# Where the loads of wo, wout and the spatial weights stand in the SyncE queue

## The chip, the cores and the metric

The kernel runs on one core of a Trainium2 chip. A core has TensorE (PE) for matrix products, VectorE (DVE), ScalarE (ACT) and GpSimd (POOL) for work on elements, and SyncE (SP), which here does nothing but issue DMA transfers. Each engine works through its own list of instructions in order; semaphores make one engine wait for another or for the landing of a transfer. The metric is the device time of one execution in microseconds; the median of several runs is compared.

## The reference

Two branches over the same x (2048 tokens of 512) are mixed with a gate for each token:

```python
q = (x @ wq) as 32 heads of 16          # keys and values: one head of 16, shared by all
scores = q k^T * 16 ** -0.5;  p = softmax(scores);  a = (p v) @ wo

z = gelu(x @ w_in)                      # 1376 wide, split into halves of 688
z1, z2 = z[..., :688], layernorm(z[..., 688:])
g = w_sp @ z2 + b_sp                    # over the tokens, w_sp is 2048 x 2048
b = (z1 * g) @ w_out

gate = sigmoid((x * gate_w).sum(-1))
out = gate * a + (1 - gate) * b
```

## The kernel before, in words

**The attention** goes by 32 units: a chunk of 512 queries and four heads each. For a tile of 128 keys TensorE computes scores of 512 queries into a bank of PSUM (tile `ps`), from `QA` and `KA`. `KA[:, 0]` holds the keys as they come from the projection, `KA[:, 1]` the same keys moved by 16 partitions, which serves the other heads of a pair. ScalarE turns most score banks into probabilities with an exponential (`P`, line 804). The rest go to VectorE and GpSimd, which replace the exponential by a polynomial (`UW`, lines 816, 823, 829); part of that polynomial is a term that is linear in the keys, so that for those tiles sums over V (`SVB`) and over products of K and V (`KTV`) can be used. TensorE then multiplies `P` and `UW` with `V`. The three engines are loaded about equally by this.

**The gMLP** is fitted into the same stream on TensorE: `win` (the first gMLP weights) gives z1 and z2, ScalarE applies the gelu, VectorE the layer norm; then `wT`, the transposed spatial weights, in four loads of 512 columns; then `wout` for the gMLP's result and `wo` for that of the attention, both added in one bank.

**What sets the order.** When the program is built, a planner plays the engines' work through with costs and due times of its own and writes out a fixed list of instructions for each engine. `op(engine, ...)` appends to the list; what an operation reads and writes determines its waits. SP's list, too, is in the order in which the planner calls `op("sp", ...)`. SP takes its list strictly in that order: where an entry waits, all behind it wait.

**The DMA helpers around the change.** `ld_K1(c, t)` (line 305) issues the copy of one chunk of 512 keys from `KA[:, 0]` to `KA[:, 1]` (line 306); it waits only for VectorE, which writes the chunk. `sp_dma` (line 282) issues a load and, with `chain=True`, makes it wait for the landing of the load that was issued by `sp_dma` before. `ld_win` loads win, `ld_bsp` (line 314) a row of 512 numbers of b_sp into `bspz`, `ld_wo` (line 317) issues eight loads of 64 KB. `ld_rest` (line 344) issues the load of wout, two small loads for the rest of wout, and `ld_wT(0)`: four transposing loads of 128 rows of w_sp each (line 339). The groups of these lists that TensorE computes have a `done` function, which the planner calls when the group is through and which appends what follows: `done` of `g_K` (the projection of the keys of one chunk, in the order of chunks 0, 3, 2, 1) appends that chunk's key copy; `done` of `g_KTV` (the sums over products of K and V) appends four small copies that spread the sums into `KTV` (lines 590 to 592), and behind them the loads of wo, wout and wT. The sums over V come as a group of their own, `g_SV`, right beside it.

In this program the group g_KTV is through before the last key chunk, chunk 1.

Of the kernel before, what the change touches and what calls it, by code (L numbers as in the profile page):

```python
# [78 lines left out]
class Prog:  # L79
# [12 lines left out]
    def op(self, eng, fn, r=(), w=(), chan=None, dma=0, after=(), tag=""):  # L92
        if dma:
            chan = "%s_d%d" % (self.name, self.ndma)
            self.ndma += 1
        else:
            chan = "%s_%s%s" % (self.name, eng, chan or "")
        o = Op(eng, fn, chan, dma, tag)
        deps = []
        for k in r:  # L100
            d = self.lastw.get(k)
            if d is not None:
                deps.append((d, True))
        for k in w:
            d = self.lastw.get(k)
            if d is not None:
                deps.append((d, True))
            for d in self.readers.get(k, ()):
                deps.append((d, False))
        for d in after:  # L110
            deps.append((d, True))
        if eng == "pool" and self.ops[eng] and not self.ops[eng][-1].dma and not dma:
            deps.append((self.ops[eng][-1], True))
        seen = set()
        for d, raw in deps:
            if d.eng == eng and not d.dma:
                if eng == "pe":
                    continue
            if id(d) in seen:
                continue  # L120
            seen.add(id(d))
            d.need = True
            o.deps.append(d)
        for k in r:
            self.readers.setdefault(k, []).append(o)
        for k in w:
            self.lastw[k] = o
            self.readers[k] = []
        self.ops[eng].append(o)
        return o  # L130
# [39 lines left out]
def build_kernel(nc, x_d, wq_d, wk_d, wv_d, wo_d, win_d, wsp_d, bsp_d, wout_d, gw_d, out_d):  # L170
    es = ExitStack()
    with es:
        block = es.enter_context(nc.Block())

        def sb(name, shape, dt):
            return es.enter_context(nc.sbuf_tensor(name, shape, dt))
# [3 lines left out]
        def bank(b, n=512, off=0):  # L180
            return ps[:, 512 * b + off:512 * b + off + n]
# [4 lines left out]
        def bkey(b):  # L186
            return ("bk", b)
# [23 lines left out]
        wo = sb("wo", [128, 4, D], B16)  # L211
# [70 lines left out]
        def sp_dma(fn, r=(), w=(), n=16, chain=True, tag=""):  # L282
            o = op("sp", fn, r=r, w=w, dma=n, after=[dprev[0]] if chain and dprev[0] is not None else [], tag=tag)
            dprev[0] = o
            return o
# [19 lines left out]
        def ld_K1(c, t):  # L305
            op("sp", lambda q: q.dma_start(KA[16:128, 1, 512 * c:512 * c + 512], KA[0:112, 0, 512 * c:512 * c + 512]),
               r=[("K0", c)] + (["K0a"] if c == XO[0] else []), w=[("K1", c)], dma=16, tag="K1")
            spc["free"] = max(spc["free"], t) + 650.0
            T[("K1", c)] = spc["free"] + 2300.0

        def ld_win():
            sp_dma(lambda q: q.dma_start(win[:], win_d.rearrange("(dt p) n -> p dt n", p=128)), w=["win"])

        def ld_bsp(tc):
            sp_dma(lambda q: q.dma_start(bspz[0:1, tc % 2, :], bsp_d[512 * tc:512 * tc + 512].rearrange("(one t) -> one t", one=1)), w=[("bspz", tc % 2)])
# [20 lines left out]
        def ld_wT(tc):  # L336
            for k in range(4):
                r0 = 512 * tc + 128 * k
                sp_dma(lambda q, r0=r0, tc=tc, k=k: q.dma_start_transpose(wT[:, :, 128 * k:128 * k + 128], wsp_d[r0:r0 + 128, :]),
                       w=[("wT", k)], tag="wT")  # L340
            if tc > 0:
                ld_bsp(tc)

        def ld_rest():
            sp_dma(lambda q: q.dma_start(wout[:, 0:5, :], wout_d[0:640, :].rearrange("(ft p) n -> p ft n", p=128)), w=["wout"])
            for h in range(2):
                sp_dma(lambda q, h=h: q.dma_start(wout[64 * h:64 * h + 48, 5 + h, :], wout_d[640:688, :]), w=["wout5"])
            ld_wT(0)
# [24 lines left out]
        def mm(dst, lhsT, rhs, start, stop, r, w, tp=None, chan=None, tag=""):  # L373
            def fn(t):
                if tp is None:
                    return t.matmul(dst, lhsT, rhs, start=start, stop=stop)
                return t.matmul(dst, lhsT, rhs, start=start, stop=stop, tile_position=tp)  # L377
            return op("pe", fn, r=r, w=w, chan=chan, tag=tag)
# [6 lines left out]
        def fm(b, n, off, lhsT, rhs, start, stop, r, tag):  # L385
            for q in range(4):
                mm(ps[32 * q:32 * q + 32, 512 * b + off:512 * b + off + n], lhsT[:, 32 * q:32 * q + 32], rhs, start, stop, r, [bkey(b)],
                   tp=(0, 32 * q), tag=tag)
# [12 lines left out]
        def when(*keys):  # L401
            t = 0.0
            for k in keys:
                if k not in T:
                    return None
                t = max(t, T[k])
            return t
# [33 lines left out]
        def qt(x):  # L441
            t = x[2]() if callable(x[2]) else x[2]
            return 1e12 if t is None else t

        def g_K(c, lo=0, hi=512, b=BM):
            key = "K0a" if c == XO[0] and lo == 0 else ("K0", c)

            def piece(dt):
                return lambda: fm(b, hi - lo, 0, wk_rep[:, dt, :], xT[:, dt, 512 * c + lo:512 * c + hi], dt == 0, dt == 3, ["wk_rep", ("x", c)], "K")

            def ev():
                op("dve", lambda v: v.tensor_copy(KA[:, 0, 512 * c + lo:512 * c + hi], bank(b, hi - lo)), r=[bkey(b)], w=[key], tag="Kev")

            def done(t):
                T[key] = t
                if hi == 512 and c == XO[1]:
                    ld_K1(c, t)
                    ld_K1(XO[0], t)
                elif hi == 512 and c == XO[2]:
                    ld_K1(c, t)  # L460
                    ld_win()
                elif hi == 512 and c == XO[3]:
                    ld_K1(c, t)
                    ld_bsp(0)
                if all(("K0", c2) in T for c2 in range(4)) and hi == 512:
                    for c2 in range(4):
                        early.append(g_k2(c2))
            return Group([((hi - lo) / 2.4 + 2.6, piece(dt)) for dt in range(4)], [(68.0 + (hi - lo) / 0.96, ev)], lambda: when(("x", c)), done, bank=b, tag="K")
# [105 lines left out]
        def g_KTV():  # L574
            n0 = NKT - NMAX

            def piece(k, e):
                def f():
                    for q in range(4):
                        o = 512 * BM + 32 * NMAX * e  # L580
                        mm(ps[32 * q:32 * q + 32, o:o + 32 * (k + 1)], KN[:, k, e, :], V1[:, n0 + k:n0 + k + 1, :].broadcast_to([128, k + 1, 32]), k == NMAX - 1, k == 0,
                           ["KN", ("V", (n0 + k) // 4)], [bkey(BM)], tp=(0, 32 * q), tag="KTV")
                return f

            def ev():
                op("dve", lambda v: v.tensor_scalar(KF, bank(BM, 64 * NMAX).rearrange("p (e k w) -> p k e w", e=2, w=32), Q_C1, None, ALU.mult),
                   r=[bkey(BM), ("z1", 5)], w=["KF"], tag="KTVev")

            def done(t):
                for q in range(4):  # L590
                    op("sp", lambda d, q=q: d.dma_start(KTV[32 * q:32 * q + 32, :, :, q, :], KF[32 * q:32 * q + 32, :, :, :]),  # L591
                       r=["KF", ("z1", 5)], w=[("KTV", q)], dma=16, after=[o_ktv], tag="KTV")
                T["KTV"] = t + 6000.0
                sp_dma(ld_wo, w=["wo"], n=128)
                ld_rest()
            return Group([(26.0 + 13.4 * k, piece(k, e)) for e in range(2) for k in range(NMAX - 1, -1, -1)], [(C_EV, ev)], lambda: when(("V", 2), ("V", 3)), done, tag="KTV")

        def gate():
# [351 lines left out]
        for i, c in enumerate(XO):  # L950
# [3 lines left out]
        free = {"pe": 6600.0, "act": 7000.0, "dve": 6800.0}  # L954

        first = deque([g_K(XO[0], 0, 128), g_Q(0, DBK[0]), g_K(XO[0], 128, 512), g_V(XO[0], BO), g_K(XO[1]), g_V(XO[1], BO), g_K(XO[2]), g_V(XO[2]),
                       g_K(XO[3]), g_V(XO[3])])
        early = deque()
# [964 lines left out]
def bass_gated_mix__grouped_kv_mqa__mixer_gmlp__prompt_kernel(  # L1923
    nc, A_x, A_wq, A_wk, A_wv, A_wo, B_x, B_w_in, B_w_sp, B_b_sp, B_w_out, gate_w, out,
):
    build_kernel(nc, A_x, A_wq, A_wk, A_wv, A_wo, B_w_in, B_w_sp, B_b_sp, B_w_out, gate_w, out)
# [29 lines left out]
```

## Time and profile before

| | us |
|---|---|
| median of 3 runs | 748.63 (748.27 to 748.7) |
| the profiled execution, its own time | 748.98 |
| its span, first to last instruction | 747.2 |
| PE busy | 714.1 (96%) |
| DVE busy | 704.9 (94%) |
| ACT busy | 708.7 (95%) |
| POOL busy | 471.3 (63%) |
| mean granted TensorE clock | 0.985 of full speed |

Times in the rows of the profile are microseconds from the span's start, unless marked ns. A row of the timeline has start, duration, engine, line, operation, output and input and the count; a bracket at the end is the idle time of the engine before it and what ended it. SPq is SP's queue with its DMA issues; the duration of such a row is that of issuing, not of the transfer. The granted clock is the share of full speed that TensorE was allowed.

### The profile page before, as it was taken

What the parts mean: (1) busy time and instruction counts of PE and PEld (TensorE: products, weight loads), DVE (VectorE), ACT (ScalarE), POOL (GpSimd) and SP (SyncE); (2) the same over time, 40 slices, a digit from 0 to 9 for tenths busy, and PEclk for the clock granted to TensorE, in tenths of its full rate; (3) what the DMA queues carried; (4) which work ended last, traced back from release to release, by engine and by line L of the source; (5) the groups of instructions that cost most, each with busy time, mean ns of one, the idle gap of its engine ahead of it and who ended that gap; (6) DMA issues with size and microseconds to landing.
All of it is one profiled execution on the core that took longest, in us unless ns stands there. A gap on an engine that the chain in (4) does not pass through costs nothing.

```text
span 747.2 us, 21846 instructions
## 1 busy us (share of the span) xinstructions
PE 714.1 (96%) x9048; PEld 210.7 (28%) x9048; DVE 704.9 (94%) x1035; ACT 708.7 (95%) x757; POOL 471.3 (63%) x440
## 2 busy tenths in 40 slices
PE   8927999999999999999999999999999999999996
PEld 3302322232432222322222232222223222222322
DVE  6934999999999999999999999999999999999996
ACT  5936999999999999999999999999999999999995
POOL 5520376766037876667777677756767776677772
PEclk9977999999999999999999999999999999999999
DMA  8441000000001000150000105000001510000101
GB/s 156 133 113 36 1 2 2 2 2 1 3 2 27 4 2 2 30 100 9 9 1 2 38 2 128 9 10 2 1 2 23 109 36 8 2 2 2 31 1 33
DMA packets 59810, 20.12 MB, mean 27 GB/s; under 512 B 54804, under 2 KB 59192, under 8 KB 59704
## 3 DMA queue, kind: packets, MB, share of 16 engines
q1 hardware_dynamic: 57448, 18.36, 11.0%
q8 instruction: 73, 1.20, 0.6%
q10 hardware_dynamic: 2256, 0.30, 0.2%
q14 instruction: 33, 0.27, 0.1%
HBM read 3.38 MB, written 2.10 MB: 7 GB/s over the span
## 4 chain that ended last, share of the span: by engine, by line
PE 69%; DVE 11%; ACT 10%; DMA 4%; issue 4%; SPq 1%; ACTq 0%; DVEq 0%
PE ps L377 69%; ACT P L804 9%; DVE UW L816 4%; DVE bst L635 2%; DMA wT<-in_B_w_sp_dram 2%; DVE UW L823 2%; DVE UW L829 1%; DMA wout<-in_B_w_out_dram 1%; DVE z L649 1%; DMA xT<-in_A_x_dram 1%; SPq L591 0%; SPq L318 0%; DMA KA<-KA 0%; ACT z L629 0%; DMA wo<-in_A_wo_dram 0%
## 5 line engine op out<-in xcount | busy, mean ns | idle before, releaser
L804 ACT ACTIVATE P<-ps 128x1024 bf16<-128x1024 f32 (+1 forms) x738 | 683.5, 1185 | 27.0 <-PE ps L377 26.7
L829 POOL TENSOR_TENSOR UW<-UW 128x512 f16<-128x512 f16 (+1 forms) x300 | 375.4, 1251 | 156.1 <-DVE UW L829 63.8
L816 DVE TENSOR_SCALAR UW<-ps 128x512 f16<-128x512 f32 (+1 forms) x423 | 351.0, 851 | 2.6 <-PE ps L377 1.9
L377 PE MATMUL ps<-QA,KA 32*128 32x512 bf16 x2048 | 313.6, 385 | 23.2 <-DMA KA<-KA 18.1
L377 PE MATMUL ps<-P,V 128*32 128x512 bf16 x1488 | 204.7, 386 | 0.4 <-issue 0.3
L823 DVE TENSOR_TENSOR UW<-UW 128x2048 f16<-128x2048 f16 (+1 forms) x176 | 177.9, 1011 | 1.3
L377 PEld LDWEIGHTS ps<-QA,KA 32*128 32x128 bf16 x2048 | 86.1, 91 | 325.6 <-ACT P L804 151.7
L377 PE MATMUL ps<-UW,VW 128*32 128x512 f16 x560 | 119.5, 384 | 0.0
L377 PE MATMUL ps<-wT,z 128*32 128x512 bf16 (+1 forms) x1536 | 116.3, 366 | 0.0
L829 DVE TENSOR_TENSOR UW<-UW 128x1024 f16<-128x1024 f16 (+4 forms) x176 | 109.0, 634 | 1.9 <-POOL UW L829 1.9
L377 PE MATMUL ps<-UW,V 128*32 128x512 f16 x560 | 83.9, 387 | 0.7 <-DVE UW L823 0.4
L377 PEld LDWEIGHTS ps<-P,V 128*32 128x32 bf16 x1488 | 46.8, 94 | 53.7 <-issue 48.7
L377 PEld LDWEIGHTS ps<-wT,z 128*32 128x32 bf16 x1536 | 28.2, 94 | 40.9 <-issue 40.4
L510 POOL TENSOR_TENSOR QSQ<-QA 128x512 bf16<-128x512 bf16 x16 | 25.7, 1609 | 19.8 <-DVE z L649 8.6
L621 DVE CAST z<-ps 128x344 bf16<-128x344 f32 x32 | 16.2, 506 | 21.2 <-PE ps L377 21.1
L377 PEld LDWEIGHTS ps<-UW,VW 128*32 128x32 bf16 x560 | 27.9, 94 | 17.3 <-issue 14.5
L377 PE MATMUL ps<-wout,z 128*32 128x512 bf16 x384 | 31.9, 384 | 0.0
L377 PE MATMUL ps<-win,xT 128*32 128x344 bf16 x512 | 30.6, 317 | 0.2 <-DVE km L488 0.2
L377 PEld LDWEIGHTS ps<-UW,V 128*32 128x32 bf16 x560 | 19.9, 95 | 19.6 <-issue 14.9
L472 POOL TENSOR_TENSOR KSQ<-KA 128x512 bf16<-128x512 bf16 x4 | 5.6, 1408 | 31.3 <-PE ps L377 31.2
L841 DVE STREAM_TRANSPOSE T<-ps 128x512 f32<-128x512 f32 (+1 forms) x33 | 22.7, 691 | 1.4 <-PE ps L377 1.3
L377 PE MATMUL ps<-QA,KTV 128*32 128x512 bf16 x128 | 23.3, 383 | 0.0
(114 smaller groups left out, 384.1 us busy)
## 6 DMA issues: line engine op xcount, KB each, us to landing
out_dram<-outsb SPq DMA_DIRECT2D x15, 128.0 KB, 1.7
win<-in_B_w_in_dram SPq DMA_DIRECT2D x1, 1376.0 KB, 7.5
wout<-in_B_w_out_dram SPq DMA_DIRECT2D x1, 640.0 KB, 4.2
wo<-in_A_wo_dram SPq DMA_DIRECT2D x8, 64.0 KB, 2.5
KA<-KA SPq DMA_DIRECT2D x4, 112.0 KB, 2.6
UW<-in_A_wq_dram SPq DMA_DIRECT2D x1, 384.0 KB, 4.1
wT<-in_B_w_sp_dram SPq DMA_TRANSPOSE x16, 4.4
UW<-in_A_wq_dram ACTq DMA_DIRECT2D x1, 128.0 KB, 3.9
```

The source lines that it names most:

```text
L377: return t.matmul(dst, lhsT, rhs, start=start, stop=stop, tile_position=tp)
L472: op("pool", lambda g: g.tensor_tensor(KSQ[:], KA[:, 0, 512 * c:512 * c + 512], KA[:, 0, 512 * c:512 * c + 512], ALU.mult), r=[("K0", c), ...
L510: dq(pl_q, 1050.0, lambda: op("pool", lambda v: v.tensor_tensor(QSQ[:, q % 2, :], QA[:, q % NQ, :], QA[:, q % NQ, :], ALU.mult), r=[("Q", ...
L621: ev = lambda: op("dve", lambda v: v.tensor_copy(z2[:, FH * st + 344 * h:FH * st + 344 * h + 344], bank(BM, 344)), r=[bkey(BM)], w=[("z2", ...
L635: dq(dve_q, 410.0, lambda st=st, h=h: op("dve", lambda v: v.bn_stats(bst[:, st, h, :], z2[:, FH * st + 344 * h:FH * st + 344 * h + 344]), ...
L649: op("pool" if st in ZP else "dve", lambda v: v.tensor_scalar(z2[:, FH * st:FH * st + FH], z2[:, FH * st:FH * st + FH], mv[:, st, 0:1], rs ...
L804: op("act", lambda a: a.activation(P[:, 512 * p0:512 * (p0 + n)], ps[:, 512 * b0:512 * (b0 + n)], ACT.Exp), r=[bkey(b0 + i_) for i_ in ran ...
L816: op("dve", lambda v: v.tensor_scalar(UW[:, 0, s, 512 * i:512 * (i + n)], bank(b, 512 * n), Q_A, Q_AS, ALU.mult, ALU.add), r=[bkey(b + j) ...
L823: op("dve", lambda v: v.tensor_tensor(src, src, src, ALU.mult), r=k, w=k, tag="dTT")
L829: op(eng, lambda v: v.tensor_tensor(UW[:, 1, s, 256 * a:256 * b], src, src, ALU.mult), r=[("U", s, h) for h in range(a // 2, (b + 1) // 2) ...
L841: return lambda: pgx.op("dve", lambda v: v.transpose(T1[:, jj, c0:c1], bank(BO, c1 - c0, c0)), r=[bkey(BO)], w=[("T1", jj, c0)], tag="T1")
```

## The change

The loads of wo, wout and the first four of wT are no longer appended by `done` of `g_KTV` alone. A counter starts at two; `done` of `g_KTV` and `done` of `g_K` for the last chunk each count it down, after appending their own transfers, and the one that brings it to zero appends the loads.

```diff
+        lates = [2]
+
+        def ld_late():
+            lates[0] -= 1
+            if not lates[0]:
+                sp_dma(ld_wo, w=["wo"], n=128)
+                ld_rest()
+
         def g_K(c, lo=0, hi=512, b=BM):
@@
                 elif hi == 512 and c == XO[3]:
                     ld_K1(c, t)
                     ld_bsp(0)
+                    ld_late()
@@ done of g_KTV
                 T["KTV"] = t + 6000.0
-                sp_dma(ld_wo, w=["wo"], n=128)
-                ld_rest()
+                ld_late()
```

The lists of TensorE, VectorE, ScalarE and GpSimd hold the same instructions in the same order with the change; only SP's list differs. Behind the change the lines of the kernel are numbered 8 or 9 higher, so that line 591 of before is line 600 of the changed kernel.

## The prediction

> **What bounds the kernel now.** I read the page's chain of waits first. In a kernel whose three compute engines are each busy for about 95% of the span, a share of the chain on DMA is a hole that all three share.
>
> ```profile
> PE 69%; DVE 11%; ACT 10%; DMA 4%; issue 4%; SPq 1%; ACTq 0%; DVEq 0%
> ```
>
> DMA has 4% of 747.2 us, about 30 us. The second view is who waited for whom between 36 and 70 us, asked once for each engine (engine, line, what it waited for: total us, times, longest us):
>
> ```profile
> PE ps L377 <- DMA KA<-KA: 18.1, 1, 18.1
> ACT P L804 <- PE ps L377: 20.3, 4, 17.8
> DVE z L621 <- PE ps L377: 21.1, 1, 21.1
> ```
>
> TensorE waits once, 18.1 us, for a copy of the keys (KA into KA); ScalarE and VectorE wait behind it. The third view is the chain in order of time, its longest pieces (start us, us, what):
>
> ```profile
> 32.45 2.35 DMA wo<-in_A_wo_dram
> 34.82 4.15 DMA wout<-in_B_w_out_dram
> 39.03 1.75 DMA wout<-in_B_w_out_dram
> 40.80 1.68 DMA wout<-in_B_w_out_dram
> 42.50 4.44 DMA wT<-in_B_w_sp_dram
> 46.96 4.24 DMA wT<-in_B_w_sp_dram
> 51.21 4.39 DMA wT<-in_B_w_sp_dram
> 55.61 1.87 SPq L339
> 57.53 2.72 DMA KA<-KA
> 60.30 6.52 PE ps L377 x48
> ```
>
> The copy itself takes 2.72 us. Everything above it is loads that SP issues one by one, each waiting for the landing of the one before, and none of which TensorE needs at that time. The copy merely stands behind them in SP's queue. The queue's own timeline (start, us, engine, line, op, transfer, count):
>
> ```profile
> 18.25 0.59 SPq L312 DMA_DIRECT2D win<-in_B_w_in_dram  x1
> 25.52 3.41 SPq L591 DMA_DIRECT2D KTV<-z  x4
> 28.98 3.90 SPq L318 DMA_DIRECT2D wo<-in_A_wo_dram  x8
> ...
> 42.50 14.98 SPq L339 DMA_TRANSPOSE wT<-in_B_w_sp_dram  x4
> 57.53 0.59 SPq L306 DMA_DIRECT2D KA<-KA  x1
> 59.95 0.28 SPq L315 DMA_DIRECT2D bspz<-in_B_b_sp_dram  x1
> ```
>
> The copy's source was ready far earlier. VectorE wrote it here (timeline of VectorE):
>
> ```profile
> 27.38 0.67 DVE L452 CAST KA<-ps 128x512 bf16<-128x512 f32 x1
> ```
>
> That ends at 28.05, while the copy is issued at 57.53: 29.5 us lost in the queue, of which TensorE had other work for all but 18.1.
>
> The last view is busy time by stretch (stretch, length, then busy us and count for PE, PEld, DVE, ACT, POOL, then granted clock, DMA share, GB/s):
>
> ```profile
> 28.93:42.20 13.27, 13.21 (x206) 4.14 (x191) 13.24 (x23) 13.27 (x16) 7.15 (x18) 1.00 0.35 103
> 42.20:60.30 18.10, 0.01 (x1) 0.01 (x1) 2.00 (x3) 0.90 (x1) 2.51 (x2) 0.60 0.55 122
> 60.30:66.87 6.57, 6.57 (x57) 1.85 (x61) 1.18 (x3) 3.50 (x3) 0.00 (x0) 0.54 0.01 3
> ```
>
> Before the hole ScalarE has no gap and VectorE and TensorE hardly any. In the hole nothing runs but 0.90 us of ScalarE and 2.00 us of VectorE left over. After it TensorE needs 6.57 us at a granted clock of 0.54. So the hole costs its 18.1 us and a second piece, the slow restart.
>
> **The change part by part.** It adds and removes no work. On SP one group of issues moves: eight wo, one wout, two wout pieces and four wT transposes go from ahead of the key copy and the bspz load to behind both.
>
> SP before, from the KTV spread (KTV<-z, the spread that the other moves refer to) to the bspz load:
>
> ```order
> L591 DMA KTV<-z 32x16x32 [waits f_dve]
> L591 DMA KTV<-z 32x16x32 x3
> L318 DMA wo<-in_A_wo_dram 16x4x512 [waits f_d12]
> L318 DMA wo<-in_A_wo_dram 16x4x512 x7
> L345 DMA wout<-in_B_w_out_dram 128x5x512 [waits f_d17]
> L347 DMA wout<-in_B_w_out_dram 48x512 [waits f_d18,f_pool]
> L347 DMA wout<-in_B_w_out_dram 48x512 [waits f_d19]
> L339 DMA_TRANSPOSE wT<-in_B_w_sp_dram 128x16x128 [waits f_d20]
> L339 DMA_TRANSPOSE wT<-in_B_w_sp_dram 128x16x128 [waits f_d21]
> L339 DMA_TRANSPOSE wT<-in_B_w_sp_dram 128x16x128 [waits f_d22]
> L339 DMA_TRANSPOSE wT<-in_B_w_sp_dram 128x16x128 [waits f_d23]
> L306 DMA KA<-KA 112x512 [waits f_dve]
> ```
>
> SP with the change, the same place:
>
> ```order
> L600 DMA KTV<-z 32x16x32 [waits f_dve]
> L600 DMA KTV<-z 32x16x32 x3
> L306 DMA KA<-KA 112x512 [waits f_dve]
> L315 DMA bspz<-in_B_b_sp_dram 1x512 [waits f_d12,f_pool]
> L318 DMA wo<-in_A_wo_dram 16x4x512 [waits f_d18]
> L318 DMA wo<-in_A_wo_dram 16x4x512 x7
> L345 DMA wout<-in_B_w_out_dram 128x5x512 [waits f_d19]
> L347 DMA wout<-in_B_w_out_dram 48x512 [waits f_d20,f_pool]
> L347 DMA wout<-in_B_w_out_dram 48x512 [waits f_d21]
> L339 DMA_TRANSPOSE wT<-in_B_w_sp_dram 128x16x128 [waits f_d22]
> ```
>
> The copy now waits for nothing but VectorE (f_dve); the loads chain behind bspz (f_d18). On TensorE the program reads, around the place of the wait, with the change:
>
> ```order
> L377 MATMUL ps<-xT,wqd 32x512 x4
> L377 MATMUL ps<-P,V 32x512 x4
> L377 MATMUL ps<-QA,KA 128x512 [waits f_act]
> L377 MATMUL ps<-QA,KA 128x512 [waits f_d17]
> L377 MATMUL ps<-P,V 32x512 x4
> L377 MATMUL ps<-CT,zer 32x512 x4
> L377 MATMUL ps<-UW,V 32x512 [waits f_dve]
> ```
>
> The second score matmul waits for the copy (f_d17; the same semaphore was f_d25). Nothing else moved there, nor on the other three compute engines.
>
> **Is the copy in time?** It is issued when the KTV issues end, 25.52 + 3.41 = 28.93. The landings of the four key copies:
>
> ```profile
> DMA to landing us min/median/max: 2.3/2.6/3.6
> ```
>
> So it lands between 31.3 and 32.6. TensorE comes to it at 42.20, about 10 us later. The wait is gone, not shortened; to return it would need a landing after 13.3 us, with four KTV copies beside it.
>
> **What the hole was worth.** Three readings bound it. TensorE's: 18.1 us of wait, and the restart, 6.57 us at 0.54, which is 6.57 x 0.54 = 3.5 us at full clock, so 3.1 us: 21.2. But ScalarE must keep up. Its rows:
>
> ```profile
> 41.49 1.61 ACT L804 ACTIVATE P<-ps 128x1536 bf16<-128x1536 f32 x1
> 60.94 1.02 ACT L804 ACTIVATE P<-ps 128x1024 bf16<-128x1024 f32 x1 [17.84 <-PE ps L377]
> 62.94 1.45 ACT L804 ACTIVATE P<-ps 128x1536 bf16<-128x1536 f32 x1 [0.98 <-PE ps L377]
> 64.89 1.02 ACT L804 ACTIVATE P<-ps 128x1024 bf16<-128x1024 f32 x1 [0.50 <-PE ps L377]
> 66.87 1.94 ACT L804 ACTIVATE P<-ps 128x1024 bf16<-128x1024 f32 x2 [0.96 <-PE ps L377]
> ```
>
> It ends its backlog at 43.10, then has three activations (3.50 us) up to the one at 66.87. Without gaps, as in 28.93 to 42.20, that one starts at 43.10 + 3.50 = 46.60: 20.3 us earlier, which is the sum of its four waits. TensorE could be there at 42.20 + 3.5 = 45.7, earlier than ScalarE, so ScalarE decides. VectorE:
>
> ```profile
> 42.99 1.21 DVE L823 TENSOR_TENSOR UW<-UW 128x2048 f16<-128x2048 f16 x1
> 65.25 0.52 DVE L621 CAST z<-ps 128x344 bf16<-128x344 f32 x1 [21.05 <-PE ps L377]
> ```
>
> It loses 21.05 us from 44.20 on, more than ScalarE, so after the hole it was the late one; running on, it has to wait for TensorE's matmuls of win for some tenths. I take 20.4, ScalarE's figure and a tenth of what VectorE was behind. Bounds: 18.1 (the wait alone) and 21.2.
>
> The Trainium skill, TensorE: Matmul & The Clock Gate, section "Part 1: The HAM clock gate", has the array halve its clock after an idle window of about 3.4 us and regain it after about as long a stretch of work. The trace agrees on the fall; its restart lasted longer (6.57 us at 0.54). By the page's figure the restart would cost an estimated 1.7 us, and the gain would be 19.8.
>
> **What the moved loads cost.** The bspz load, about 1 KB, has no landing of its own in the trace; the smaller wout pieces took 1.75 and 1.68, so wo starts about 29.6 + 0.3 + 1.7 = 31.6 instead of 28.98, and the last wT load, which now is in at about 42.50 + 4 x 4.4 = 60, is in at about 63. If bspz took twice as long, 2 us more. Who needs them (first and last start in the rows of these tiles):
>
> ```profile
> L377 PE MATMUL ps<-wT,z x1536: 272/379/393, 222.1 to 707.2; 128*32 128x512 bf16 x160, 128*32 128x256 bf16 x32
> L377 PE MATMUL ps<-bspz,ones x96: 272/379/391, 221.9 to 702.9; 128*32 128x512 bf16 x80, 128*32 128x256 bf16 x16
> ```
>
> After the shift the first is near 201.5, so there are some 138 us of slack; wout and wo are used with the results, later still. Behind these loads on SP comes the transpose of OT, which waits for GpSimd far later. What is new is that the four wT transposes run beside full compute instead of in a hole. The later three sets do that already. Two of them, each with the stretch behind it:
>
> ```profile
> 313.37:330.10 16.73, 16.73 (x201) 4.35 (x197) 16.37 (x24) 16.73 (x19) 10.92 (x11) 1.00 0.66 117
> 332.20:349.00 16.80, 16.80 (x195) 4.43 (x188) 16.70 (x24) 16.80 (x20) 12.44 (x12) 1.00 0.08 25
> 447.65:464.50 16.85, 16.85 (x204) 4.56 (x202) 16.62 (x25) 16.85 (x20) 13.45 (x14) 1.00 0.57 125
> 465.00:482.00 17.00, 17.00 (x196) 4.54 (x194) 16.89 (x24) 17.00 (x20) 12.99 (x11) 1.00 0.08 25
> ```
>
> With the loads TensorE does 201 and 204 matmuls, without them 195 and 196; VectorE's gaps differ by 0.2 to 0.3 us. I cost the overlap at nothing, from -0.3 to +0.3.
>
> Sum: the profiled execution took 748.98 (span 747.2, and 1.8 around it). 748.98 - 20.4 = 728.6. The median of the runs is 748.63, 0.35 less: **728.2**.
>
> **The rivals.** (a) Only the wait is won. If ScalarE's short waits of 0.98, 0.50 and 0.96 are due to the order of TensorE's program (matmuls of win and of zeros stand between the scores) and not to the clock, they stay: 748.63 - 17.84 = 730.8. For it: ScalarE's and TensorE's work in that stretch are equal (3.5 and 3.5), so no slack. Against: the same mix ran at 13.27 of 13.27 before the hole.
>
> (b) A new wait that the hole covered, on GpSimd: it idled there too and could be behind. It was busy only 7.15 of 13.27 us before the hole, and in 42.20 to 60.30 it finished within 2.51 us. If 2.51 us of backlog each were to hold up the key norms and the squares of the queries, 5 us come back: 733.
>
> (c) Slower. The wT transposes share the 16 DMA engines with everything else, the engines' fetches of instructions included; if these starve, the engines halt for as long as the transposes run. Four of them at about 4.4 us each last 17.4 us; halting throughout gives back 17.4 of 20.4 (745.6). Only if that stretch takes over 2.2 times its length (17.4 + 20.4 over 17.4) does the kernel get slower: at 2.4 times it is 17.4 x 1.4 = 24.4 us longer, 4.0 more than won, 752.6. The rows of 313 to 464 speak against any of it. The Trainium skill, DMA: Bandwidth & Descriptors, section "Queues, rings and completion order", lets each DMA engine alternate between queues packet by packet; by that rule fetches are delayed, not starved, and the trace agrees (TensorE 16.73 of 16.73 at a DMA share of 0.66).
>
> (d) The change does not do what it says: the copy is still held on SP, by KTV or its semaphore, past 60: no change, 748.6. The order shows only KTV ahead of it.
>
> **How the numbers follow.** My forecast, 727.0 to 729.5, gets 0.72; (a), 729.5 to 731.5, 0.15; (b) 0.07; below 727.0, where VectorE's lag is won as well, 0.02; (c) and (d) 0.02 each. The range of 726.8 to 731.0 takes in the bounds of the gain (21.2 gives 727.4, 18.1 gives 730.5) and the overlap's 0.3 on both sides, and holds about 0.84. Differences within 0.2% (1.5 us) cannot be told from no change here: faster 0.96, same 0.02, slower 0.02.
>
> **What would show it.** In the changed profile: the key copy is issued near 29 and no row of TensorE waiting for KA remains; the granted clock stays at 1.00 from 28 to 100; ScalarE has no gap above 1 us between 40 and 50; wT transposes are issued from about 45 to 60 under full compute; the first read of wT falls near 201.5. I am wrong in the main step if TensorE stops between 40 and 60 for another reason, wrong in the restart if ScalarE still shows gaps of about 1 us there at full clock, and wrong on the cover if the matmul counts per us fall while wT loads run.

## The result, and the profile after

The changed kernel took a median of 728.09 us (727.49 to 730.03 in four runs) against 748.66 us of the kernel before beside it (748.27 to 749.78): a ratio of 0.9727, with a 95% interval of 0.9706 to 0.9749. The forecast was 728.2, with a range of 726.8 to 731.0.

SP's queue of the changed kernel, with its columns as before:

```profile
27.54 3.54 SPq L600 DMA_DIRECT2D KTV<-z  x4
31.13 0.63 SPq L306 DMA_DIRECT2D KA<-KA  x1
31.85 0.43 SPq L315 DMA_DIRECT2D bspz<-in_B_b_sp_dram  x1
33.33 4.04 SPq L318 DMA_DIRECT2D wo<-in_A_wo_dram  x8
39.13 0.39 SPq L345 DMA_DIRECT2D wout<-in_B_w_out_dram  x1
43.32 2.08 SPq L347 DMA_DIRECT2D wout<-in_B_w_out_dram  x2
48.09 16.60 SPq L339 DMA_TRANSPOSE wT<-in_B_w_sp_dram  x4
```

The key copy, issued at 57.53 before, is now issued at 31.13, and the wT loads are issued from 48 to 65. Who waited for whom between 20 and 70 us, the longest waits of TensorE and ScalarE and those of VectorE:

```profile
PE ps L377 <- ACT P L812: 0.7, 4, 0.2
ACT P L812 <- PE ps L377: 1.3, 3, 0.5
DVE UW L824 <- PE ps L377: 0.7, 1, 0.7
DVE z L629 <- PE ps L377: 0.6, 1, 0.6
```

TensorE's wait of 18.1 us for KA is gone, and nothing of that size came in its place. In the chain of waits the share of DMA fell from 4% to 1%, and what is left of it is the load of x at the start:

```profile
PE 74%; ACT 12%; DVE 9%; issue 3%; DMA 1%; ACTq 0%; DVEq 0%
```

This profiled execution was the longest of the four, 730.03. It shows a stretch near the start, ahead of the changed place, that the profiled execution of before does not have (busy time by stretch; the third column from the right is the granted clock):

```profile
12.00:14.00 2.00, 1.88 (x76) 0.81 (x74) 1.70 (x6) 2.00 (x3) 1.82 (x4) 0.90 1.19 119
14.00:16.00 2.00, 2.00 (x12) 0.47 (x14) 1.44 (x3) 1.50 (x2) 1.77 (x5) 0.50 0.90 229
16.00:20.00 4.00, 4.00 (x33) 0.60 (x25) 2.54 (x4) 3.23 (x4) 0.58 (x2) 0.50 0.01 2
20.00:25.00 5.00, 5.00 (x151) 2.49 (x152) 4.56 (x11) 4.53 (x5) 2.83 (x4) 0.96 0.84 271
```

At half clock from about 14 to 20 us TensorE ran late, so that the KTV copies start at 27.54 instead of 25.52. Event by event the two traces are therefore best compared in a later execution of the changed kernel, e12 below (728.22, clock 1.00 from the start). There the first product with wT starts here:

```profile
L377 PE MATMUL ps<-wT,z x1536: 272/379/393, 201.7 to 686.8; 128*32 128x512 bf16 x160, 128*32 128x256 bf16 x32
```

It was 222.1 before: 20.4 of the 20.8 us between these two executions (748.98 and 728.22) are won ahead of that point, and the other 0.4 behind the last of these products (707.2 before, 686.8 now).

### The profile page after: what moved, and what is told of

It is laid out like the page before. It is cut to its first block, busy times and chain, and to the rows that moved or that the text cites. A ratio compares the mean times of both kernels' runs of the same rounds, so it can differ in the third digit from the quotient of the medians.

```text
span 728.2 us, 21847 instructions
## 1 busy us (share of the span) xinstructions
PE 713.6 (98%) x9048; PEld 210.3 (29%) x9048; DVE 705.1 (97%) x1035; ACT 708.6 (97%) x757; POOL 471.4 (65%) x440
## 4 chain that ended last, share of the span: by engine, by line
PE 74%; ACT 12%; DVE 9%; issue 3%; DMA 1%; ACTq 0%; DVEq 0%
PE ps L377 74%; ACT P L812 12%; DVE UW L824 3%; DVE bst L643 2%; DVE UW L831 1%; DVE UW L837 1%; DVE z L657 1%; DMA xT<-in_A_x_dram 1%; ACT z L637 0%; DVE T L849 0%; DVE mv L647 0%; DVE z L729 0%; ACT L637 0%; DVE rc L867 0%; DVE Tn L877 0%
## 5 line engine op out<-in xcount | busy, mean ns | idle before, releaser
L377 PEld LDWEIGHTS ps<-UW,V 128*32 128x32 bf16 x560 | 19.8, 94 | 19.2 <-issue 14.4
L377 PE MATMUL ps<-CT,SVB 128*32 128x512 bf16 x128 | 23.2, 385 | 0.0
L377 PE MATMUL ps<-xT,win 128*32 128x512 bf16 (+1 forms) x384 | 22.3, 363 | 0.5 <-ACT P L812 0.5
```

## The experiments

The kernel before ran beside every group of them: medians of 749.06 (e2, e3, e4, e8), 749.46 (e1, e5, e6, e7) and 750.66 (e9 to e12).

**e8 and e12: the changed kernel again**, as partner on the same chips. No edit.

> The changed kernel once more, to have it on the same chip as the kernels below. All theories: 728.1, within 727 to 730. The profile of the first run showed the clock at 0.50 from about 13.8 to 20.4 us, before the place of the change, and that run took 730.0, while the three others took 727.5 to 728.5 at a mean clock of 0.997 to 0.998. If that dip is a matter of chance at the start, runs with a mean clock of 0.997 or more take 727.5 to 728.5, and runs at 0.994 take about 2 us more. If it belongs to the change, every run has it.

> The changed kernel, partner of the run before on the same chip: 728.1, within 727.4 to 730.1, with a run now and then at a mean clock of about 0.994 and 2 us longer.

Measured: e8 728.19 (727.82 to 728.9), ratio 0.972 (0.9704 to 0.9736); e12 727.99 (727.49 to 728.64), ratio 0.9698 (0.9685 to 0.971). None of these nine executions had a mean clock under 0.998, so the dip at 14 us in the first profile is not part of the change. The forecast of an occasional run at 0.994 was not met here.

**How the stall depends on what stands ahead of the copy: e1, e2, e3, e4.** Each leaves another part of the loads ahead of the key copy.

```diff
 done of g_KTV, before ld_late():
 e1:  + ld_wo, the large wout load
 e2:  + ld_wo, all wout loads
 e3:  + ld_wo, all wout loads, ld_wT(0) k = 0
 e4:  + ld_wo, all wout loads, ld_wT(0) k = 0, 1
 ld_late() then issues what is left
```

> Part of the move: the eight wo loads and the large wout load stay ahead of the last key copy, the small wout loads and the four wT transposes go behind it. Copy issued at 34.82 + 0.43 = 35.3, landing 38.0, TensorE needs it at 42.2. Main theory: in time by 4 us, as good as the whole change, 728.1. Rival (the copy must come directly behind the KTV copies, or the margin of 10 us is not real): a wait of some us, above 730.

> Half of the move: wo and all of wout stay ahead of the last key copy, only the four wT transposes go behind it. From the rows of the kernel before the copy is then issued at 41.2 (right after the last small wout load at 40.80 + 0.33) and lands 2.7 later, 43.9; TensorE is there at 42.2. Main theory (the copy's place in the queue sets the stall, and a restart at half clock comes on top only when the clock has had time to fall, which in the kernel before was 3.7 us after TensorE stopped): a wait of 1.7 us, no fall of the clock, ScalarE loses about 1.3: 728.1 + 1.3 = 729.4. Rival (only the wT transposes matter, by their own traffic): no wait, 728.1.

> As the last, with one of the four wT transposes ahead of the key copy. Copy issued at 42.50 + 1.95 = 44.5, landing 47.2, TensorE waits 5.0 us. The clock should fall 3.7 us into the wait, so a restart follows. Main theory: the restart costs as much as in the kernel before (20.4 lost for a wait of 18.1: 2.3 more), 5.0 + 2.3 = 7.3 lost: 735.4. Rival (a) of the prediction, the wait alone: 728.1 + 4.7 = 732.8.

> As the last, with two of the four wT transposes ahead of the key copy. Copy issued at 46.96 + 1.95 = 48.9, landing 51.6, TensorE waits 9.4 us. Main theory: 9.4 + 2.3 = 11.7 lost: 739.8. Rival (a), the wait alone: 728.1 + 9.1 = 737.2. If the loss were in proportion to the loads moved (two of four, half of 20.4), 738.3.

| kernel | TensorE's wait for KA in the profile | ScalarE's waits for TensorE there | VectorE's longest wait there | median | above 728.1 |
|---|---|---|---|---|---|
| e1 | none | 0.3 | 0.8 | 727.98 | -0.1 |
| e2 | 2.3 | 4.9 | 5.1 | 729.65 | 1.6 |
| e3 | 5.5 | 7.4 | 8.3 | 736.61 | 8.5 |
| e4 | 9.9 | 10.8 | 12.3 | 740.52 | 12.4 |
| before | 18.1 | 20.3 | 21.1 | 748.66 | 20.6 |

The waits of e2 are those of its longest execution, 732.98; the other profiled executions lie within 0.4 us of their medians.

(The ratios to the kernel before: e1 0.9708, 0.969 to 0.9726; e2 0.9733, 0.9717 to 0.975; e3 0.9828, 0.9809 to 0.9848; e4 0.9894, 0.9869 to 0.9919.)

SP's queue in e1 (the copy and its neighbours):

```profile
34.63 0.38 SPq L605 DMA_DIRECT2D wout<-in_B_w_out_dram  x1
35.05 0.58 SPq L306 DMA_DIRECT2D KA<-KA  x1
39.38 0.29 SPq L315 DMA_DIRECT2D bspz<-in_B_b_sp_dram  x1
```

The copy is issued at 35.05, as forecast, but runs beside the wout load, and took this long to land (transfer, queue, count, KB, us):

```profile
KA<-KA SPq DMA_DIRECT2D x1, 112.0 KB, 4.4
```

So it was in at 39.5, still ahead of TensorE, and cost nothing. It is not the place right behind KTV that counts, but being in before 42. From e3 on, the loss is the wait and about 2.5 to 3 us more, as the main theory had it (735.4 and 739.8 forecast, 736.6 and 740.5 measured); the wait alone (732.8 and 737.2) is too little, and so is a loss in proportion to the loads moved (738.3 for e4). In e2 the forecast of no fall of the clock held for three of five executions, at a mean clock of 0.999: 729.20 to 729.65. One at 0.996 took 731.25, and the one that was profiled, at 0.994, took 732.98. Its waits and its clock (stretches of 1 us):

```profile
PE ps L377 <- DMA KA<-KA: 2.3, 1, 2.3
```

```profile
42.00:43.00 1.00, 0.09 (x1) 0.00 (x0) 1.00 (x2) 0.99 (x1) 0.80 (x1) 1.00 0.16 48
43.00:44.00 1.00, 0.00 (x0) 0.00 (x0) 1.00 (x2) 0.00 (x0) 0.82 (x1) 0.76 0.39 116
44.00:45.00 1.00, 0.62 (x5) 0.19 (x9) 0.23 (x1) 0.00 (x0) 1.00 (x1) 0.50 0.00 1
```

The profiled execution, with its restart at half clock, took 3.3 to 3.8 us more than the three at 0.999. In it the copy was also issued at 42.1 instead of the 41.2 of the forecast, so up to 0.9 of that may be wait, if the others had the copy as forecast; they have no trace. The rest is the restart: it has a price of its own, and after a short wait it comes in some executions only.

**e5: the hole of before, filled.**

```diff
 def s_mm(...):                       # the kernel before
+    ahead of the first score matmul that needs chunk 1 of KA[:, 1]:
+        80 x mm(bank(dst_bank), zer[:], CT[:], True, True)
```

> The kernel before with the queue as it was, and 80 matmuls of zeros (128 x 512, some 0.22 us each, 17.3 us in all) on TensorE right ahead of the score matmul that waits for the key copy, into the bank that this matmul overwrites. The wait for the copy stays, but TensorE is busy for most of it, so that the clock should stay at 1.00 through the hole. Main theory: the restart is a matter of the clock, and its 2.3 us are won: 748.6 - 2.3 = 746.3, and ScalarE's waits of 0.98, 0.50 and 0.96 behind the hole are gone. Rival (a): they come from the order of TensorE's list and stay: 748.6 (at the most 0.3 less).

Measured: 748.44 (746.47 to 752.29 in twelve runs), ratio 0.9995 (0.9977 to 1.0013): no difference from the kernel before can be told, the forecast of 746.3 was missed, and by its number rival (a)'s 748.6 was met. What speaks on the mechanism is the profile of one execution (747.13). TensorE, ScalarE and the clock in it:

```profile
41.94 17.44 PE L376 MATMUL ps<-CT,zer 128*128 128x512 bf16 x80
61.39 0.38 PE L377 MATMUL ps<-QA,KA 32*128 32x512 bf16 x1 [2.02 <-DMA KA<-KA]
```

```profile
40.40 2.51 ACT L810 ACTIVATE P<-ps 128x1024 bf16<-128x1024 f32 x2
61.81 9.01 ACT L810 ACTIVATE P<-ps 128x1024 bf16<-128x1024 f32 x8 [18.91 <-PE ps L377]
```

```profile
59.20:61.00 1.80, 0.18 (x1) 0.00 (x0) 0.00 (x0) 0.00 (x0) 0.00 (x0) 1.00 0.93 219
61.00:63.00 2.00, 1.61 (x21) 0.58 (x25) 0.00 (x0) 1.06 (x2) 0.00 (x0) 1.00 0.00 1
```

The clock stays at 1.00, and ScalarE, after its one long wait, runs eight activations without a gap; its waits of 0.98, 0.50 and 0.96 are gone. Rival (a) said that the order of TensorE's list causes them; with the same order and a full clock they are not there. The hole was longer in this execution: the copy was in 1.1 us later and TensorE was there 0.3 earlier, so it is 61.39 - 41.94 = 19.45 us instead of 18.1, which takes back 1.35 of the gain. This execution took 19.2 us more than e1 beside it (727.98), no more than its hole, while the kernel before loses 20.6 for a hole of 18.1. Five of the twelve executions took 750.7 to 752.3; why is open, since only one has a trace, and so is why the median shows no gain.

**e9 and e10: the same with a shorter hole**, to see the price of the restart apart. e10 is e4 again; e9 is e4 with 40 of the zero matmuls.

```diff
 def s_mm(...):                       # e4
+    40 x mm(bank(dst_bank), zer[:], CT[:], True, True)   at the place of e5
```

> Two of the four wT transposes ahead of the key copy, as before, and 40 matmuls of zeros (8.7 us) on TensorE in the hole that this leaves, right ahead of the score matmul that waits for the copy. The wait for the copy is the same, 9.9 us from TensorE's last work to the copy's landing, but the clock should stay at 1.00. Main theory (a restart at half clock comes on top of the wait): 2 to 3 us less than the same kernel without the fillers, 740.5 - 2.5 = 738.0. Rival (a), the wait alone: the same, 740.5.

> Two of the four wT transposes ahead of the key copy, no fillers: the partner of the run before on the same chip. All theories: 740.5, as measured before (740.1 to 743.4).

Measured: e10 740.55 (739.62 to 741.1, mean clock 0.989 to 0.991); e9 740.04, but in two heaps: three executions at a mean clock of 0.999 and 1.0 took 737.26, 737.59 and 738.03, three at 0.992 to 0.996 took 742.04, 743.62 and 743.82. By the medians alone rival (a)'s 740.5 was met; the lower heap lies at the 738.0 of the main theory. The profiled one is of the upper heap:

```profile
43.00:50.00 7.00, 7.00 (x35) 3.15 (x33) 1.20 (x2) 0.00 (x0) 1.95 (x1) 1.00 0.35 77
51.00:54.00 3.00, 0.00 (x0) 0.00 (x0) 0.00 (x0) 0.00 (x0) 0.00 (x0) 1.00 0.93 204
54.00:55.00 1.00, 0.69 (x9) 0.33 (x13) 0.00 (x0) 0.27 (x1) 0.00 (x0) 0.94 0.02 1
55.00:58.00 3.00, 3.00 (x33) 0.79 (x21) 0.00 (x0) 2.21 (x2) 0.00 (x0) 0.50 0.29 64
58.00:59.00 1.00, 1.00 (x19) 0.33 (x16) 0.31 (x1) 0.53 (x1) 0.00 (x0) 0.85 1.28 291
```

Here the copy came late (the wT loads ahead of it were issued from 45.07 on, in e10 from 43.22), the fillers ended 3.5 us before it, and the clock fell after all. Where the clock held, the gain over e10 is 740.55 - 737.59 = 3.0 us, which fits the price of a restart. But the executions of the lower heap have no trace: their copy may have landed earlier too, so e9 does not show that price by itself. The split by the clock was made after the runs.

**e6: the queue or the traffic.** The kernel before, with the last key copy on ScalarE's queue.

```diff
 def ld_K1(c, t):
-    op("sp", ...)
+    op("act" if c == XO[3] else "sp", ...)
```

> The kernel before with SP's loads in their old order, all four wT transposes in the old place, and only the last key copy issued from ScalarE's queue instead of SP's. Main theory (the copy was held by its place in SP's list, not by the traffic of the loads): it lands in time, no wait, 728.1, and up to 0.7 more for ScalarE's time to issue it: 728.1 to 728.8. Rival (the loads' traffic itself keeps the copy or TensorE): a good part of the 20 us stays, over 735.

Measured: 728.91 (728.19 to 729.57), ratio 0.972 (0.9702 to 0.9737). With the loads in their old order on SP the whole gain is there, within 0.8 us. The copy's issue on ScalarE, and the work around it:

```profile
23.61 3.89 ACT L804 ACTIVATE P<-ps 128x1024 bf16<-128x1024 f32 x4
27.73 0.60 ACTq L306 DMA_DIRECT2D KA<-KA  x1
28.45 2.43 ACT L804 ACTIVATE P<-ps 128x512 bf16<-128x512 f32 x3 [0.96 <-PE ps L377]
```

The copy shares the DMA engines with the KTV copies and the first wo loads (issued from 28.47 on), lands after 2.7 us as it did before, and is in time; TensorE's longest wait between 30 and 72 is 0.3 us, with the wT transposes running from 43.17 on. What held the copy was its place in SP's list.

**e7: does the overlap cost anything?** The changed kernel with the first set of wT loaded six times.

```diff
 ld_late():
     ld_rest()
+    for _ in range(5): ld_wT(0)
```

> The changed kernel with the first set of four wT transposes loaded six times over (the same data into the same place, five sets more), all beside full compute, from about 48 to 150 us, and done before the first read near 202. Main theory: transposes beside compute cost nothing: 728.1, with up to 0.3 for each of the five sets from what the rows of before leave open, 726.6 to 729.6. Rival (c) in a mild form: if one set costs the 0.4 us or more that would explain a difference between the forecast and the result, 730 or more.

Measured: 728.49 (727.79 to 729.45), ratio 0.9715 (0.9697 to 0.9733), against 728.19 and 727.99 of the changed kernel on two other occasions and 727.98 of e1 beside it. Its queue, and the busy time of the stretch with the loads:

```profile
46.87 115.96 SPq L339 DMA_TRANSPOSE wT<-in_B_w_sp_dram  x24
```

```profile
48.00:150.00 102.00, 99.53 (x1277) 31.25 (x1269) 100.64 (x137) 101.67 (x111) 60.61 (x51) 1.00 0.54 110
```

The same stretch of e12, in which the loads end near 65.5:

```profile
48.00:150.00 102.00, 99.53 (x1281) 31.29 (x1278) 100.63 (x137) 101.67 (x111) 60.34 (x51) 1.00 0.12 22
```

At 4.5 times the DMA share VectorE and ScalarE do the same number of instructions, TensorE four of 1281 fewer, and a few matmul records can be missing from a trace. Five more sets cost at most some tenths together: the overlap is free at what can be measured here.

**e11: an attempt at the dip near the start.** 16 matmuls of zeros in TensorE's wait of 0.8 us for ScalarE near 10 us.

```diff
 def s_mm(...):                       # the changed kernel
+    ahead of the fifth score matmul:
+        4 x fm(BM, 512, 0, zer[:], CT[:], False, False)
```

> The changed kernel with 16 matmuls of zeros (four at a time, 0.9 us in all) on TensorE in its 0.8 us of waiting for ScalarE near 10 us, where the one run at a mean clock of 0.994 had its clock fall to 0.50 from 13.8 to 20.4 us. If that fall comes from too little work on TensorE in that stretch, it becomes rarer: the slowest runs (730.0 of the first four) go, the median stays at 728.1 or falls by up to 0.5. If it is a matter of chance elsewhere, no difference to the changed kernel without the fillers.

Measured: 730.05 (728.95 to 731.81), ratio 0.9726 (0.9711 to 0.974), 2.1 us more than e12 beside it, at mean clocks of 0.994 to 0.998. It is the opposite of what was meant. TensorE in its profile (731.81):

```profile
10.23 1.03 PE L377 MATMUL ps<-CT,zer 128*32 128x512 bf16 x16
...
12.17 0.61 PE L377 MATMUL ps<-wvg,xT 128*32 128x33 bf16 x58
14.31 0.24 PE L377 MATMUL ps<-wvg,xT 128*32 128x33 bf16 x6 [1.52 <-issue]
```

The fillers fill the gap, but at 12.78, 1.5 us behind the last of them, TensorE stops for 1.52 us in the midst of 64 equal small matmuls, for nothing that the profile shows, and the clock falls behind that. What stops it is open. No kernel of this study is faster than the changed one by more than the spread of its runs (e1's 727.98 is 0.1 us less).

## Why the prediction was right

**The cause** was right: the wait for the key copy bounded that part, the copy was held by its place in SP's list (e6), and with the copy early the wait is gone, not shortened (e1, e6, e12).

**The copy in time.** In e12 the issue is at 28.68, as forecast (28.93). The margin of 10 us was real: e1 uses up 6.4 us of it, and 1.8 more for a slower landing, and loses nothing.

**What the hole was worth.** Forecast 20.4: 18.1 of wait and 2.3 for the restart. Measured 20.6 by the medians and 20.4 by the first product with wT. That the restart is a term of its own, and comes from the clock, was the contested part: e3 and e4 lose 8.5 and 12.4 us for waits of 5.5 and 9.9, and in e5 the short waits of ScalarE go with the low clock. In e12, with TensorE's list unchanged and the clock at 1.00, they are gone too. So rival (a), 730.8, falls. The size of the term was a matter of the execution: 2.3 in the sum, 2.5 in the kernel before, 2.5 to 3.0 in e3 and e4, 2.4 to 3.8 in e2. In the kernel before the clock took 6.0 us of work to return, in e2 5.9, but 4.2 in e3 and 3.5 in e4 (the rows stand in the last section). Half of that work time would be 3.0 us before, 2.1 in e3 and 1.8 in e4, against 2.5, 3.0 and 2.5 above the wait: that there is a term follows from the clock, its size in each kernel does not, and stays open. The Trainium skill, TensorE: Matmul & The Clock Gate, section "Part 1: The HAM clock gate", has at least one busy window of about 3.4 us for the return; with one window the term would be an estimated 1.7 and the gain 19.8. The 3.5 us of e4 agree with that, the 6.0 of the kernel before do not. The 95% interval of the result, a gain of 18.8 to 22.0 us, holds 19.8 as well as 20.4, so the medians do not decide between the two; the 17.8 of rival (a) lie outside it.

**That ScalarE decides** is not shown. In e12 ScalarE waits 0.3 us in all between 36 and 70, so the gapless run that the sum assumed is what happened. But ScalarE's 20.3 us of before, less these 0.3, are 20.0, while VectorE's 21.1, less the 0.7 that it still waits in e12 for TensorE's matmuls of win (the "some tenths" of the forecast), are 20.4, the gain by the first product with wT between the same two executions. In e3 and e4, too, VectorE's waits (8.3 and 12.3) come closer to the losses of 8.5 and 12.4 than ScalarE's (7.4 and 10.8). These rows point to VectorE rather than ScalarE as what set the loss; no run separates the two. That ScalarE's figure and a guessed tenth of VectorE's lag gave 20.4 is in part luck.

**The moved loads.** wo was expected at 31.6 and starts at 31.40 in e12; the bspz load took 1.5 us to land instead of 1.7. SP's queue of e12:

```profile
31.40 4.47 SPq L318 DMA_DIRECT2D wo<-in_A_wo_dram  x8
...
42.01 2.08 SPq L347 DMA_DIRECT2D wout<-in_B_w_out_dram  x2
47.07 16.87 SPq L339 DMA_TRANSPOSE wT<-in_B_w_sp_dram  x4
```

The wT loads start at 47.07, not at 45: from the first small wout load to the first wT load it is 5.1 us here and was 3.5 before. Their issues take 16.87 instead of 14.98, and the last load is in near 65.5, not at 63. Whether compute beside them is the reason is not shown; in e1, also beside full compute, they take 15.36. None of it matters with the first read at 201.7 (forecast 201.5). That the overlap is free (from -0.3 to +0.3) is borne out by e7, and rival (c) falls with it. (The prediction read VectorE's gaps with and without loads as 0.2 to 0.3 us apart; by its rows they are 0.26 and 0.12 apart, which changes nothing.) The rule of the Trainium skill, DMA: Bandwidth & Descriptors, "Queues, rings and completion order", by which a DMA engine takes its queues in turn, packet by packet, so that fetches beside transfers would be delayed and not starved, agrees with e7: TensorE is busy for 99.53 of 102 us at a DMA share of 0.54. That the queues take turns is shown by no run here.

**Rivals (b) and (d).** No wait on GpSimd or elsewhere above 0.7 us shows in that part for the three compute engines, and the copy is issued right behind the KTV copies.

What the prediction did not have: the profiled execution was forecast at 728.6 and took 730.03, because of the dip at 14 us, which is not at the changed place. And e5, an expectation with a definite number, missed it: I took the length of the hole as fixed, while it is set by a chain of landings, and lasted 1.35 us longer in the one execution with a trace; what kept the median from gaining stays open.

## What to carry to other kernels

A queue that issues in order is a list like that of any engine: ask of each entry how soon its landing is needed, and put a short transfer that is needed soon ahead of long chained loads that are needed late; here the order of one queue cost 20 us with every engine's own program unchanged. A hole that all engines share costs more than its length if TensorE's clock falls in it, by 2 to 4 us here, so read the granted clock behind it before you count its worth. And where executions of one kernel fall into two heaps, sort them by the mean granted clock before you believe a median; here that told them apart in e2 and e9, while in e5 the clocks of the longer executions (0.994 to 0.997) and of the others (0.996 to 0.999) overlap.

## What the runs showed that was not expected

**The clock was low for whole multiples of about 3.4 us.** From the granted clock of short stretches the moments of its fall and return can be worked out: a stretch of 1 us at a mean of 0.91 was at 1.00 for 0.82 us and at 0.50 for 0.18, since the stretches beside it show these two values alone. Fall and return in the kernel before:

```profile
45.00:46.00 1.00, 0.00 (x0) 0.00 (x0) 0.00 (x0) 0.00 (x0) 0.09 (x1) 0.91 1.29 275
66.00:66.50 0.50, 0.50 (x11) 0.10 (x3) 0.36 (x1) 0.00 (x0) 0.00 (x0) 0.71 0.00 0
```

In e2 TensorE's last matmul ahead of its wait and the first behind it:

```profile
41.70 0.38 PE L377 MATMUL ps<-QA,KA 32*128 32x512 bf16 x1
44.38 0.60 PE L377 MATMUL ps<-QA,KA 32*128 32x512 bf16 x1 [2.29 <-DMA KA<-KA]
```

The fall is in the row of 43 to 44 above, the return here:

```profile
50.00:52.00 2.00, 2.00 (x26) 0.42 (x18) 1.57 (x3) 1.07 (x2) 0.38 (x1) 0.92 0.54 113
```

In e3, with TensorE's first matmul behind the wait:

```profile
45.00:46.00 1.00, 0.00 (x0) 0.00 (x0) 0.00 (x0) 0.00 (x0) 0.03 (x1) 0.54 1.24 256
51.00:52.00 1.00, 1.00 (x13) 0.10 (x3) 0.00 (x0) 0.74 (x1) 0.00 (x0) 0.55 1.27 286
```

```profile
47.65 0.60 PE L377 MATMUL ps<-QA,KA 32*128 32x512 bf16 x1 [5.52 <-DMA KA<-KA]
```

In e4, the same:

```profile
45.00:46.00 1.00, 0.00 (x0) 0.00 (x0) 0.00 (x0) 0.00 (x0) 0.02 (x1) 0.64 1.21 258
55.00:56.00 1.00, 1.00 (x17) 0.26 (x7) 0.00 (x0) 1.00 (x1) 0.00 (x0) 0.74 1.12 245
```

```profile
51.98 0.60 PE L377 MATMUL ps<-QA,KA 32*128 32x512 bf16 x1 [9.88 <-DMA KA<-KA]
```

The rows of e9 stand with that experiment.

| kernel | fall | return | low for | in steps of 3.41 |
|---|---|---|---|---|
| before | 45.82 | 66.29 | 20.5 | 6.0 |
| e2 | 43.52 | 50.32 | 6.8 | 2.0 |
| e3 | 45.08 | 51.90 | 6.8 | 2.0 |
| e4 | 45.28 | 55.52 | 10.2 | 3.0 |
| e9 | 54.88 | 58.30 | 3.4 | 1.0 |

The step is worked out from the table (20.47 / 6 = 3.41). The delay of a fall, on the other hand, has no fixed length: in e2 the clock fell 1.4 us after TensorE's last matmul had ended (42.08), in the kernel before after 3.6, and in e5 TensorE stood for 2.0 us without a fall. It looks as if the clock were judged at the ends of steps that run on by themselves; then the price of a hole would depend on where in a step it begins and ends, which differs between executions. No run moved a hole within a step, so this stays an inference. It agrees with the free-running window that the Trainium skill describes in the section named above; but its idle window of about 3.4 us is not needed for a fall: in e2 it came after 1.4 us, in a stop of 2.3.

**A fall without a hole.** In the first profile of the changed kernel the clock was at half from about 14 to 20 us, a low of about two steps again, though TensorE had been busy for 1.88 of the 2 us in which it fell. TensorE had waited 0.8 us for ScalarE some 3 us earlier; the executions without the dip had that wait too. Whether the place of the step decides was not tried.

**A stop of TensorE that nothing explains** in e11, 1.5 us between equal matmuls, after 16 matmuls had been added ahead of it. What causes it stays open.
